# Polysketch attention with an exact-GELU MLP: every engine put into written order, and the opening laid out anew

## Chip, cores, metric

One core of one Trainium2 chip. The metric is the device time of one launch in microseconds, in medians of several runs. Each ratio is to runs of the kernel before on the same chip in the same rounds. A difference in us between two changed kernels is one of medians; a1, a2, b1 and b2 ran on another chip than the other experiments, but the kernel before took 338.88 us on the one and 338.78 to 338.85 on the other.

## The reference, cut to what matters

```python
def _attn_ref(q, k, v, S1, S2):                 # batch 4, heads 4, seq 1088, head_dim 32, r = 8
    def phi(x):                                 # 64 features: products of two 8-wide sketches
        a = np.einsum('rd,bhsd->bhsr', S1, x)
        b = np.einsum('rd,bhsd->bhsr', S2, x)
        return np.einsum('bhsi,bhsj->bhsij', a, b).reshape(*x.shape[:-1], r * r)
    q_p, k_p = (phi(q), phi(k))
    kv = np.einsum('bhsf,bhsd->bhfd', k_p, v)   # the key sums
    z = np.sum(k_p, axis=2)
    num = np.einsum('bhsf,bhfd->bhsd', q_p, kv)
    den = np.einsum('bhsf,bhf->bhs', q_p, z)[..., None] + 1e-06
    return (num / den).astype(np.float32)       # the division
# then x (4352 x 128): h = x @ w_in (128 x 2048); g = exact gelu(h); out = g @ w_out (2048 x 128)
```

The weights and sketches come as 64-bit floats and are converted on the chip by integer arithmetic ("conversion" below).

## The kernel before, in the parts that the argument touches

The 1088 tokens of each batch are two main chunks of 512 positions and a remainder of 64. There are nine chunks in all (the ninth holds the remainders). The MLP takes a chunk in 16 steps; a step is one hidden product, one gelu and one output product. Attention of the next chunk and the keys of the next batch are placed in slots between the steps.

TensorE (PE) makes the matrix products and transposes; VectorE (DVE), ScalarE (ACT) and GpSimd (POOL) do the elementwise work; SyncE (SP) issues loads. The results of TensorE land in PSUM banks and are copied or multiplied out of them. Names in the profiles: kT is a tile of transposed keys, from which and from the sketches (S) TensorE makes the key features, k_p; "expand" makes the query sketches (w_ps<-qT,Srep), whose products are q_pT (ACT copies one factor, A_sb, out of PSUM for that); kz or kv are the key sums; den is the denominator; xT is the divided, transposed attention output that the hidden products read. A pass is one of the two instructions of an fp32 product. At full pace the two passes of a 128x512 product take 0.86 us; "half pace" is about 1.8 us for the same.

```python
        def transposes(srcs):                       # keys: transpose, then copy out of PSUM on DVE
            ...
            nc.vector.tensor_copy(out=T["kT"][:, :n * 128], in_=ps[:, :n * 128])
        def features(n, pair=None):                 # needs kT
            ps = work_bank()
            for i in range(n):
                nc.tensor.matmul(ps[:, i * 64:(i + 1) * 64], lhsT=T["kT"][:, i * 128:(i + 1) * 128],
                                 rhs=S12.rearrange("p h r -> p (h r)"), start=True, stop=True)
            ...
        def num_over_den():                         # the division, features on the partitions
            ...
            for h in range(H):
                nc.scalar.activation(out=den[h * D:(h + 1) * D, :W], in_=banks[r][at:at + D, :W],
                                     func=ACT.Copy, bias=1e-6)
            nc.vector.reciprocal(out=den[:, :W], in_=den[:, :W])          # 128x512
            for h in range(H):
                nc.vector.tensor_mul(out=xT[n][rows, :W], in0=banks[h % 2][rows, :W], in1=den[rows, :W])
    ...
    for f in key_stages(0) + chunk_queries(0):
        f()
    round_bits(w_in_sb[0])                          # eight DVE instructions for each weight tile
    ...  # in the loop: chunk n+1's three query stages in slots 1, 3, 6; the next batch's keys from slot 7
```

This is the order as written. In the kernel before it isn't what runs: the framework's scheduler reorders each engine's instructions.

## Time and profile before

| | kernel before |
|---|---|
| time, median of 4 runs | 338.91 us (338.67 to 338.97) |
| span of the profiled run | 337.1 us |
| first hidden product starts | 41.93 us |
| TensorE without any gap | 70.6 to 331 us |

The profile is read by stretch: where TensorE is busy without a gap at full pace, nothing but less TensorE work helps; where it has gaps, the engine named as the releaser sets the time. The lines are in the prediction below. "PEld" is the weight load, "x8" counts instructions, and the bracket at the end of a line is the idle time before it and who ended it.

### The profile page before, as it was taken

The page shows a single profiled execution, that of the slowest core. Times are in us where ns is not written, and L with a number is a line of the kernel's source. Part 1 is how long each engine was busy: PE and PEld are TensorE (multiplying, and loading weights), DVE is VectorE, ACT ScalarE, POOL GpSimd, SP SyncE. Part 2 cuts the span into 40 slices and gives each one's busy share as a digit, 9 for nine tenths or more (in the row PEclk, how much of TensorE's full clock was granted, in tenths as well). Part 3 has the DMA queues.
Part 4 walks back from the last instruction along what each step waited for, and adds up shares of the span by engine and source line. Part 5 has one row for each costly group of instructions (what it writes and reads, how often), then busy time and mean ns, then how long its engine had stood idle before and what let it go on. Part 6 is the DMA issues. An engine that isn't in the chain of part 4 may idle for free.

```text
span 337.1 us, 2831 instructions
## 1 busy us (share of the span) xinstructions
PE 308.6 (92%) x1059; PEld 154.9 (46%) x1059; DVE 150.8 (45%) x276; ACT 125.4 (37%) x227; POOL 6.0 (2%) x21
## 2 busy tenths in 40 slices
PE   1895099799999999999999999999999999999993
PEld 1881033356434444664344435744444344444682
DVE  2348999994347054723470249124522470430101
ACT  1003137213273346222553373125533643443340
POOL 2002000000000000000000000000000000000000
PEclk9999999979999999999999999999999999999998
DMA  5999400000000000000000000000000000000000
GB/s 154 296 370 348 128 0 0 0 0 2 31 1 0 0 33 0 0 1 2 31 0 0 31 2 0 0 0 34 0 0 20 13 0 0 31 0 2 0 31 16
DMA packets 13852, 13.29 MB, mean 39 GB/s; under 512 B 3856, under 2 KB 12304, under 8 KB 13840
## 3 DMA queue, kind: packets, MB, share of 16 engines
q1 hardware_dynamic: 13840, 13.13, 12.0%
q8 instruction: 8, 0.13, 0.1%
q14 instruction: 4, 0.03, 0.0%
HBM read 10.90 MB, written 2.23 MB: 39 GB/s over the span
## 4 chain that ended last, share of the span: by engine, by line
PE 84%; DVE 13%; DMA 1%; issue 0%; SPq 0%; ACT 0%; DVEq 0%
PE o_ps L334 34%; PE h_ps L325 32%; PE kv_ps L216 6%; PE w_ps L193 3%; PE w_ps L267 3%; DVE q_pT L280 2%; PE w_ps L288 2%; DVE den L296 2%; PE w_ps L345 2%; DVE bits_e L123 1%; DVE bits_m L118 1%; PE w_ps L259 1%; PE w_ps L186 1%; DMA raw_SR<-in_S_dram 1%; DVE bits_e L122 1%; DVE xT L300 1%
## 5 line engine op out<-in xcount | busy, mean ns | idle before, releaser
L325 PE MATMUL h_ps<-xT,w_in 128*128 128x512 f32 (+1 forms) x288 | 143.3, 583 | 8.2 <-DVE xT L300 8.0
L334 PE MATMUL o_ps<-g,w_out 128*128 128x512 f32 (+1 forms) x288 | 142.7, 580 | 2.0 <-DVE w_out L124 2.0
L328 ACT ACTIVATE g<-h_ps 128x512 f32<-128x512 f32 (+1 forms) x144 | 82.4, 574 | 153.3 <-PE h_ps L325 151.7
L325 PEld LDWEIGHTS h_ps<-xT,w_in 128*128 128x128 f32 x288 | 54.6, 193 | 68.7 <-issue 49.6
L334 PEld LDWEIGHTS o_ps<-g,w_out 128*128 128x128 f32 x288 | 51.5, 191 | 55.0 <-issue 49.5
L296 DVE RECIPROCAL den<-den 128x512 f32<-128x512 f32 (+1 forms) x9 | 28.6, 3174 | 33.3 <-ACT den L294 33.3
L280 DVE TENSOR_TENSOR q_pT<-A_sb,w_ps 64x256 f32<-64x256 f32 x64 | 27.1, 424 | 18.3 <-ACT A_sb L273 17.0
L261 DVE COPY qT<-w_ps 128x512 f32<-128x512 f32 (+1 forms) x9 | 6.0, 662 | 54.1 <-PE w_ps L259 54.0
L273 ACT COPY A_sb<-w_ps 64x512 f32<-64x512 f32 (+1 forms) x36 | 19.1, 553 | 17.5 <-PE w_ps L267 10.3
L300 DVE TENSOR_TENSOR xT<-w_ps,den 32x512 f32<-32x512 f32 (+1 forms) x36 | 23.6, 657 | 0.9
L294 ACT ACTIVATE den<-w_ps 32x512 f32<-32x512 f32 (+1 forms) x36 | 20.3, 565 | 6.7 <-PE w_ps L288 6.3
L216 PEld LDWEIGHTS kv_ps<-v_aug,k_p 128*128 128x128 f32 x128 | 19.6, 226 | 6.8 <-issue 5.2
L216 PE MATMUL kv_ps<-v_aug,k_p 128*128 128x66 f32 x128 | 19.4, 305 | 0.4 <-DVE k_p L204 0.4
L338 DVE COPY o_sb<-o_ps 128x512 f32<-128x512 f32 (+1 forms) x9 | 6.0, 662 | 26.8 <-PE o_ps L334 26.8
L204 DVE TENSOR_TENSOR k_p<-a_t,w_ps 128x256 f32<-128x256 f32 x32 | 11.7, 416 | 11.4 <-ACT a_t L197 11.3
L288 PE MATMUL w_ps<-q_pT,kz 64*64 64x512 f32 (+1 forms) x96 | 10.8, 523 | 3.8 <-DVE q_pT L280 3.8
L193 PEld LDWEIGHTS w_ps<-S,kT 128*128 128x128 f32 x68 | 10.7, 233 | 5.6 <-DVE kT L188 4.0
L193 PE MATMUL w_ps<-S,kT 128*128 128x64 f32 x68 | 11.4, 318 | 1.3 <-DVE kT L188 1.3
L197 ACT COPY a_t<-w_ps 128x128 f32<-128x128 f32 (+1 forms) x10 | 2.5, 249 | 26.4 <-PE w_ps L193 26.4
L267 PE MATMUL w_ps<-qT,Srep 32*128 32x512 f32 (+1 forms) x72 | 10.8, 671 | 0.0
L188 DVE COPY kT<-w_ps 128x512 f32<-128x512 f32 (+1 forms) x10 | 6.1, 610 | 7.1 <-PE w_ps L186 7.0
L347 DVE COPY oT<-w_ps 128x512 f32<-128x512 f32 (+1 forms) x9 | 6.0, 662 | 6.5 <-PE w_ps L345 6.5
(54 smaller groups left out, 94.2 us busy)
## 6 DMA issues: line engine op xcount, KB each, us to landing
k<-in_k_dram SPq DMA_DIRECT2D x4, 512.0 KB, 9.3
v<-in_v_dram SPq DMA_DIRECT2D x4, 512.0 KB, 8.8
q<-in_q_dram SPq DMA_DIRECT2D x4, 512.0 KB, 9.7
raw_w_in<-in_moe_w_in_dram SPq DMA_DIRECT2D x4, 512.0 KB, 7.2
raw_w_out<-in_moe_w_out_dram SPq DMA_DIRECT2D x4, 512.0 KB, 8.1
out_dram<-oT SPq DMA_DIRECT2D x8, 256.0 KB, 2.0
k_rem<-in_k_dram SPq DMA_DIRECT2D x4, 32.0 KB, 3.8
v_rem<-in_v_dram SPq DMA_DIRECT2D x4, 32.0 KB, 2.4
```

The lines of the kernel that those rows point to most:

```text
L193: nc.tensor.matmul(ps[:, i * 64:(i + 1) * 64], lhsT=T["kT"][:, i * 128:(i + 1) * 128], rhs=S12.rearrange("p h r -> p (h r)"), start=True, ...
L216: nc.tensor.matmul(T["kv"][:, hp * 2 * C:(hp + 1) * 2 * C], lhsT=lhs[:, hp * 128:(hp + 1) * 128], rhs=rhs[:, 2 * hp:2 * hp + 2, :], start= ...
L267: nc.tensor.matmul(banks[g][:, :W], lhsT=Srep[rows].rearrange("p a i j -> p (a i j)"), rhs=T["qT"][rows, :W], start=True, stop=True)
L273: nc.scalar.copy(out=A[F:, :W], in_=banks[g][:F, :W])
L280: nc.vector.tensor_mul(out=qp[r * F:(r + 1) * F, :, g * 128:(g + 1) * 128], in0=a3[:, r::2, :], in1=b3[:, r::2, :])
L288: nc.tensor.matmul(banks[r][c * F:(c + 1) * F, c0:c1], lhsT=kz[b][r * F:(r + 1) * F, c, :], rhs=T["qp"][r * F:(r + 1) * F, c, c0:c1], star ...
L294: nc.scalar.activation(out=den[h * D:(h + 1) * D, :W], in_=banks[r][at:at + D, :W], func=ACT.Copy, bias=1e-6)
L296: nc.vector.reciprocal(out=den[:, :W], in_=den[:, :W])
L300: nc.vector.tensor_mul(out=xT[n][rows, :W], in0=banks[h % 2][rows, :W], in1=den[rows, :W])
L325: nc.tensor.matmul(ps[:, :W], lhsT=w_tile(w_in_sb, fi), rhs=xT[n][:, :W], start=True, stop=True)
L328: nc.scalar.activation(out=g_of[n, fi][:, :W], in_=ps[:, :W], func=ACT.Gelu)
L334: nc.tensor.matmul(o_of[n][:, :W], lhsT=w_tile(w_out_sb, fi), rhs=g_of.pop((n, fi))[:, :W], start=(fi == 0), stop=(fi == NF - 1))
```

## The change

Its intent: start the MLP sooner, and keep the scheduler from reordering DVE's queue in the first 70 us. Every engine now runs in written order. Sketches, the keys' remainder and the first queries load on ACT's queue; keys go by head pair; the first two chunks are divided by token, which needs only small reciprocals, and their MLP steps are interleaved four by four; the conversion is five DVE instructions and two of ACT. Four smaller parts: POOL makes the sketch copies and two of the first key products, each key batch's sums are one burst, the PSUM banks are shared out anew, and the remainders load in two issues in place of four. The diff, cut to its core:

```diff
+class InOrder:
+    def __getattr__(self, name):
+        op = getattr(self.engine, name)
+        return lambda *a, **k: self.tc.keep_in_program_order(op(*a, **k))
...
+    pe, dve, act, pool, sp = (InOrder(tc, e) for e in (nc.tensor, nc.vector, nc.scalar, nc.gpsimd, nc.sync))
...
+        act.dma_start(out=S_dst[i * R:(i + 1) * R, :].rearrange("r (h d) -> r h d", h=H), ...)
+    load_main(sp, "k", 0, 0, 2)
+    load_main(sp, "k", 0, 2, 4)
+    load_rem(act, "k")
+    load_main(act, "q", 0)
+    load_main(sp, "v", 0)
...
+        if helped:                                   # conversion: two of seven instructions on ACT
+            act.activation(out=low, in_=lo, func=ACT.Copy, scale=2.0 ** -52)
+            ts(out=e, in0=hi, scalar1=20, scalar2=0x7FF, op0=AX.logical_shift_right, op1=AX.bitwise_and)
+            act.activation(out=r, in_=e, func=ACT.Relu, scale=2.0 ** 23, bias=below[:rows])
+        ts(out=a, ...); stt(out=m, in0=a, scalar=2.0 ** -20, in1=low, ...)
+        stt(out=e, ...); dve.tensor_mul(out=dst, in0=m, in1=e.bitcast(FP))
...
+    query_expand(0)                                  # the opening, in written order
+    ps = work_bank()
+    for hp in range(NP):
+        kv_sum(0, ps, hp)
+    kv_sum_rem(0, ps)
+    ...                                              # two ACT copies into kv0
+    query_turn(1, hidden_bank(), by_act)
+    round_bits(w_in_sb[0], 0, 256)
+    attend_by_token(0, [out_bank(), out_bank()])
+    turn_x(0, hidden_bank(), by_act)
+    query_expand(1)
...
+    steps = [(n, fi) for f in range(0, NF, 4) for n in range(2) for fi in range(f, f + 4)]
+    steps += [(n, fi) for n in range(2, NCHUNK) for fi in range(NF)]
...
+    at(0, round_bits, w_out_sb[0], 0, 256)
+    at(1, round_bits, w_in_sb[0], 256, 256)
+    at(2, lambda: attend_by_token(1, [work_bank(), work_bank()]))
+    at(3, lambda: turn_x(1, work_bank(), by_act))
+    at(3, round_bits, w_out_sb[0], 256, 256)
+    for i in range(1, d_ff // LC):
+        at(8 * i - 3, round_bits, w_in_sb[i])
+        at(8 * i - 1, round_bits, w_out_sb[i])
+    for b in range(1, B):
+        t = NCH * b * NF
+        at(t - 24, widen_v, b)
+        for hp in range(NP):
+            at(t - 23 + 2 * hp, turn_keys, b, hp)    # transposes, kT copy on DVE
+            at(t - 22 + 2 * hp, features, b, hp)
+        if b == 1:
+            at(t - 19, turn_keys_rem, b)
+            at(t - 18, features_rem, b)
+        at(t - 16, finish_keys, b)
+    for n in range(2, NCHUNK):
+        t = n * NF
+        at(t - 13, turn_queries, n)
+        at(t - 12, query_expand, n)
+        at(t - 8, attend, n)
```

## The prediction

> **What bounds the kernel now.** I read the busy time by stretch first, then the time lines of each engine. The columns of the stretches are: width, busy us (and instructions) of PE, PEld, DVE, ACT and POOL, granted clock, DMA share, GB/s.
>
> ```profile
> 0.00:41.90 41.90, 21.33 (x88) 16.12 (x88) 24.74 (x56) 6.57 (x12) 4.92 (x19) 1.00 0.83 261
> 41.90:70.60 28.70, 26.48 (x65) 10.24 (x66) 28.33 (x56) 11.63 (x20) 0.00 (x0) 0.95 0.00 0
> 70.60:331.00 260.40, 260.38 (x906) 128.38 (x905) 96.90 (x164) 107.22 (x195) 1.10 (x2) 1.00 0.02 9
> 331.00:337.10 6.10, 0.44 (x2) 0.20 (x2) 0.85 (x2) 0.00 (x0) 0.00 (x0) 0.73 0.08 22
> ```
>
> From 70.6 to 331 us TensorE has no gap: 260 us that only less TensorE work would shorten. So everything to be won lies in the first 70 us: 41.9 us before the first hidden-layer matmul, then 28.7 us in which DVE is full (28.33 of 28.70) with the weight conversion and TensorE works below its pace. That pace, in the chain of work in order of time, is 0.86 us for the two passes of one 128x512 product, so 1.72 us for a step of one hidden and one output product. The TensorE time line of the start:
>
> ```profile
> 19.96 3.52 PE L216 MATMUL kv_ps<-v_aug,k_p 128*128 128x66 f32 x16
> 23.41 1.12 PE L216 MATMUL kv_ps<-v_rem_aug,k_p_rem 64*128 64x66 f32 x4
> 24.46 2.09 PE L267 MATMUL w_ps<-qT,Srep 32*128 32x512 f32 x8
> 30.33 2.52 PE L288 MATMUL w_ps<-q_pT,kz 64*64 64x512 f32 x8 [3.78 <-DVE q_pT L280]
> ...
> 41.93 5.40 PE L325 MATMUL h_ps<-xT,w_in 128*128 128x512 f32 x6 [8.03 <-DVE xT L300]
> 47.17 1.02 PE L334 MATMUL o_ps<-g,w_out 128*128 128x512 f32 x2
> 48.03 1.02 PE L325 MATMUL h_ps<-xT,w_in 128*128 128x512 f32 x2
> ...
> 66.42 1.12 PE L334 MATMUL o_ps<-g,w_out 128*128 128x512 f32 x2 [1.97 <-DVE w_out L124]
> 67.38 1.69 PE L325 MATMUL h_ps<-xT,w_in 128*128 128x512 f32 x2
> 68.87 1.91 PE L334 MATMUL o_ps<-g,w_out 128*128 128x512 f32 x2
> ```
>
> Until about 47 us TensorE runs at half pace, though the granted clock reads 1.00: the eight L267 passes take 2.09 us here and 1.14 us at 48.98, six hidden passes 5.40 us. The 1.97 us idle at 66.4 us, waiting for a converted weight, is followed by 3.4 us at half pace. In the second stretch these are lost: 2.7 (slow first passes) + 2.2 (idle) + 2.0 (slow again) = 6.9 us.
>
> **What the Trainium skill says.** "TensorE: Matmul & The Clock Gate", Part 1, says that TensorE starts at half clock, needs about 3.4 us of sustained work to reach full clock, and falls back after an idle window of about 3.4 us. The trace agrees on the length (3.4 us slow after the gap), but a gap of 1.97 us was enough, and 7.4 us of unbroken transposes and key sums (19.1 to 26.5) did not warm it. Part 1's "Engine queue depths" says that only TensorE looks ahead, and only for weight loads, while ACT and DVE are strict FIFO: the written order is what they run, and no trace so far contradicts it. "GPSIMD Engine Reference" § 3.1 measures a two-input fp32 product of 2048 elements at 4497 ns, so I estimate about 1.1 us for each of the two 512-element products that move to POOL; the trace has none. "DMA: Bandwidth & Descriptors", "Issuing engines are not separate DMA queues", says that a second issuing engine saves issue time only.
>
> **The change, part by part.**
>
> *Two queues and the key order.* The sketch matrices now leave first, on ACT's queue; before they were the second load and landed at 5.2 us. I give 1.2 us. SyncE no longer spends 5.3 us (eight issues of 0.67 us) on the small remainders ahead of the query load. Rounding of SR stays eight small DVE instructions, 1.7 us, so features can start near 7 us, before 9.2.
>
> *The opening in written order*, at the slow pace of the old trace. Features of pair 0: 8 passes, 2.0, to 9; query transposes 0.9; features of pair 1: 2.0, to 11.5; remainder transpose and features with their copies 1.2, to 12.7; expand 2.1, to 14.8. Expand now precedes the key sums, so the eight q_pT products (8 x 0.445 = 3.6 us, DVE) lie beside them. The key sums take their PSUM bank from expand's first, free near 14.8: 32 passes x 0.235 + 4 x 0.28 = 8.5, to 23.3. Then two ACT copies and the transposes of chunk 1: 1.0. Division by token: 16 passes of 66 columns, as key sums 3.8, to 28.1. DVE then needs, for its last bank, an add, a small reciprocal and one 128x256 product, some 0.8 us, in place of ACT den 2.4 + reciprocal 3.35 + xT 2.8 = 8.5 us. Four transposes 1.0, to 29.9, and the expand of chunk 1 stands in order ahead of the first hidden product: 2.1, **to 32 us**. Gain at that mark: 41.9 - 32 = 9.9 us.
>
> *Shorter conversion, interleaved chunks.* Per weight tile DVE falls from 5 x 0.34 + 3 x 0.60 = 3.5 us to 2 x 0.34 + 3 x 0.60 = 2.5 us, two passes of 0.6 us go to ACT, and each tile lasts eight steps (13.7 us) where it lasted four. DVE stops being the bound. But at the start DVE runs the eight products of chunk 1 (to about 35) before two half tiles (2 x 1.45): the third hidden product cannot start before 37.7, the second ends at 35.5. With the slow pace around that gap and the 16 short passes of chunk 1's division, I charge 7 us (5 to 10), where the old kernel lost 6.9. So interleaving gains little net.
>
> *Dense work.* From the old loop: 331.0 - 41.9 = 289.1, less 6.9 lost = 282.2; chunk 1's transposes, expand and attend (2.5) leave, its division by token and transposes (2.2) come: **282 us**. Keys do the same passes.
>
> *Program order everywhere.* This I take as the costly part. Attend of chunk 2b-1 stands at step 32b-24; the transposes of batch b's keys at 32b-23, their features at 32b-22. For b = 2 and 3 both meet. The DVE time line of the old kernel at that place:
>
> ```profile
> 132.21 3.35 DVE L296 RECIPROCAL den<-den 128x512 f32<-128x512 f32 x1 [4.66 <-ACT den L294]
> 135.60 0.69 DVE L188 COPY kT<-w_ps 128x512 f32<-128x512 f32 x1
> 136.20 2.78 DVE L300 TENSOR_TENSOR xT<-w_ps,den 32x512 f32<-32x512 f32 x4
> ```
>
> The old schedule slipped the kT copy between reciprocal and products and let TensorE run two more steps before the features (136.34, which is 7.7 us after attend began at 128.65). In written order the kT copy stands behind both: attend 1.1 + den 2.4 + reciprocal 3.35 + xT 2.8 + copy 0.7 = 10.4 us after attend begins. TensorE is there after attend 1.0 + transposes 0.44 + four products at 0.86 = 4.9 us, and cannot pass. **Idle 5.5 us, twice**, and after each some 2 us of slow pace, as at 67 us: 15 us. For batch 1 the remainder's copy stands behind a tile's conversion at the same step, which waits for ACT: about 2 us once.
>
> *Sum.* 32 + 282 + 7 + 15 + 2 = 338; the end (o_sb copy, transposes, store) is unchanged, 6.1: span 344 us; measured time is 1.75 us above the span (338.85 against 337.1): **346 us** with the waits, **331** if the 15 us do not appear.
>
> **The rivals.** *First: the order waits are not there or shrink.* For it: whoever placed the steps by hand may have looked for just such gaps. Against: DVE is a queue, and the copy is written behind the reciprocal. Time: 331, and 327 if the opening also starts at 29. *Second: the half pace is worse than I reckon.* The key sums of a batch become one burst of 36 short passes (36 x 0.108 = 3.9 us); such passes did not warm TensorE before, so a burst could count as idle and slow the next 3.4 us. Against: 2.6 us of key passes and features at 141.4 left the clock at full. Three times 1.7 us: up to 351. *Third: the opening waits for POOL or a load.* POOL's products have 6.6 us of room before the second half of the key sums, and v landed at 7.1 before; it would move 32 by at most 3 us.
>
> **Range and chances.** I give the waits 65%: 346, give or take 5. Without them 331, give or take 4. 0.65 x 346 + 0.35 x 331 = 340.75; I say **341 us**, range **326 to 350**. Over 2% faster means below 332.1: most of the half of the second case, and a little of the first if the opening is much better: 0.30. Within 2% (332.1 to 345.6): 0.45. Slower: 0.25.
>
> **What would show it.** First hidden product at 30 to 34 us; key sums still near 0.23 us a pass, with q_pT beside them; no 3.35 us reciprocal before it. DVE no longer full from 40 to 70. Two TensorE gaps of about 5.5 us ahead of key features, released by the DVE copy of kT, at steps 42 and 74 (near 122 and 197 us: 32, plus 1.72 us a step and what is placed between), each followed by a lower granted clock. If TensorE is as unbroken after 70 us as now, the order part is wrong and the time is near 331. If the first hidden product comes after 36, the opening part is wrong.

## The result, and the profile after

**Slower by 4.3%:** 353.41 us (352.69 to 353.66, 4 runs) against 338.91; the ratio is 1.0426, with a 95% interval of 1.0408 to 1.0444. Ratios here are the mean time of one kernel's runs over the mean of the other's runs of the same rounds, so not quite the ratio of the medians. The outputs are correct.

The busy time by stretch of the changed kernel, cut where its gaps are (columns as in the prediction; rows of full pace and the end left out):

```profile
0.00:34.30 34.30, 24.93 (x108) 20.02 (x108) 10.85 (x33) 8.21 (x17) 9.34 (x37) 1.00 1.01 316
34.30:51.60 17.30, 11.45 (x39) 6.20 (x35) 10.02 (x30) 7.65 (x16) 0.00 (x0) 0.80 0.02 4
51.60:131.00 79.40, 76.75 (x256) 36.47 (x257) 38.65 (x69) 35.82 (x65) 1.10 (x2) 1.00 0.02 7
131.00:150.00 19.00, 13.58 (x44) 7.50 (x43) 10.03 (x11) 4.98 (x10) 0.00 (x0) 0.82 0.00 0
...
208.00:228.00 20.00, 14.57 (x44) 8.08 (x44) 10.05 (x11) 4.88 (x11) 0.00 (x0) 0.83 0.00 0
...
```

The MLP starts at 34.35 us, where it started at 41.93. But TensorE, which had no gap after 70.6 us, now has two of more than 5 us, one in 131 to 150 and one in 208 to 228, and each of these stretches has a granted clock near 0.82. TensorE's six longest waits, summed over the run (engine, tile, whom it waited for: us in total, times, longest):

```profile
PE w_ps L24 <- DVE kT L24: 10.8, 2, 5.4
PE h_ps L24 <- DVE w_in L24: 6.3, 2, 5.3
PE h_ps L24 <- DMA k<-in_k_dram: 4.0, 1, 4.0
PE h_ps L24 <- DMA q<-in_q_dram: 1.9, 1, 1.9
PE w_ps L24 <- DVE kT_rem L24: 1.7, 1, 1.7
PE w_ps L24 <- ACT A_sb L24: 1.6, 1, 1.6
```

All lines carry L24, the line of the in-order helper, so one goes by tiles. The first of the two kT gaps, in TensorE's and then DVE's time line:

```profile
129.56 1.09 PE L24 MATMUL w_ps<-q_pT,kz 64*64 64x512 f32 x8
...
133.70 1.02 PE L24 MATMUL h_ps<-xT,w_in 128*128 128x512 f32 x2
140.15 1.97 PE L24 MATMUL w_ps<-S,kT 128*128 128x64 f32 x8 [5.42 <-DVE kT L24]
141.91 2.02 PE L24 MATMUL o_ps<-g,w_out 128*128 128x512 f32 x2
143.72 1.69 PE L24 MATMUL h_ps<-xT,w_in 128*128 128x512 f32 x2
```
```profile
133.12 3.35 DVE L24 RECIPROCAL den<-den 128x512 f32<-128x512 f32 x1 [6.39 <-ACT den L24]
136.58 2.79 DVE L24 TENSOR_TENSOR xT<-w_ps,den 32x512 f32<-32x512 f32 x4
139.40 0.69 DVE L24 COPY kT<-w_ps 128x512 f32<-128x512 f32 x1
```

The kT copy stands behind the reciprocal and the products, as written. The transposes that it copies began at 132.4; DVE stood idle 6.39 us before 133.12, waiting in order for den. After the gap the features take 1.97 us in place of about 1.0, and the next two products 1.8 and 1.5 us (from start to start) in place of 0.86.

**Where the time went.** I took what is lost from the time line of the profiled run, as elapsed time less the same instructions at full pace. The full-pace TensorE work that is left after the first hidden product is then the same in both kernels within 0.4 us (282.2 and 281.8):

| after the first hidden product | before | after |
|---|---|---|
| start of it | 41.93 | 34.35 |
| lost to waits and half pace in the first MLP steps | 6.9 | 9.1 |
| two kT gaps (2 x 5.42) and slow passes behind (2.4 and 3.3) | 0 | 16.6 |
| waits for the remainder's kT (1.7) and for w_in at 97 us (1.0) | 0 | 2.7 |
| end (last store) | 6.1 | 6.2 |

The differences sum to -7.6 + 2.2 + 16.6 + 2.7 + 0.1 = 14.0 us; the spans differ by 350.7 - 337.1 = 13.6. (Added again from the starts in the time line, the 6.9 of the kernel before is 6.6, which changes nothing in the argument.)

### The profile page after: what moved, and what is told of

It reads as the page before. It is cut to its first block, busy times and chain, and to the rows that moved or that the text cites. A ratio compares the mean times of both kernels' runs of the same rounds, so it can differ in the third digit from the quotient of the medians.

```text
span 350.7 us, 2876 instructions
## 1 busy us (share of the span) xinstructions
PE 315.9 (90%) x1083; PEld 164.0 (47%) x1083; DVE 130.4 (37%) x236; ACT 133.1 (38%) x247; POOL 11.5 (3%) x41
## 4 chain that ended last, share of the span: by engine, by line
PE 83%; DVE 9%; ACT 4%; DMA 2%; issue 1%; ACTq 1%; DVEq 0%
PE o_ps L24 34%; PE h_ps L24 32%; PE w_ps L24 17%; DMA q<-in_q_dram 2%; DVE den L24 2%; DVE xT L24 2%; ACT den L24 1%; DVE q_pT L24 1%; ACT A_sb L24 1%; DVE bits_e L24 1%; DVE bits_m L24 1%; ACTq L24 1%; DVE w_in L24 1%; ACT g L24 0%; ACT bits_low L24 0%
## 5 line engine op out<-in xcount | busy, mean ns | idle before, releaser
L24 PE MATMUL h_ps<-xT,w_in 128*128 128x512 f32 (+1 forms) x288 | 143.7, 582 | 6.3 <-DVE w_in L24 6.3
L24 PE MATMUL o_ps<-g,w_out 128*128 128x512 f32 (+1 forms) x288 | 144.3, 584 | 0.5 <-DVE w_out L24 0.5
L24 ACT ACTIVATE g<-h_ps 128x512 f32<-128x512 f32 (+1 forms) x144 | 82.4, 573 | 158.4 <-PE h_ps L24 158.0
L24 PEld LDWEIGHTS h_ps<-xT,w_in 128*128 128x128 f32 x288 | 55.5, 194 | 73.1 <-issue 61.6
L24 PEld LDWEIGHTS o_ps<-g,w_out 128*128 128x128 f32 x288 | 51.6, 193 | 49.6 <-issue 47.3
L24 DVE TENSOR_TENSOR q_pT<-A_sb,w_ps 64x256 f32<-64x256 f32 x68 | 28.8, 424 | 25.0 <-ACT A_sb L24 23.8
L24 DVE RECIPROCAL den<-den 128x512 f32<-128x512 f32 (+1 forms) x7 | 21.9, 3124 | 40.9 <-ACT den L24 40.9
L24 DVE COPY o_sb<-o_ps 128x512 f32<-128x512 f32 (+1 forms) x9 | 6.0, 662 | 55.9 <-PE o_ps L24 55.9
L24 PEld LDWEIGHTS w_ps<-v_aug,k_p 128*128 128x128 f32 x128 | 18.1, 227 | 4.6 <-issue 4.6
L24 ACT COPY A_sb<-w_ps 64x512 f32<-64x512 f32 (+1 forms) x36 | 17.4, 557 | 6.0 <-PE w_ps L24 6.0
L24 PE MATMUL w_ps<-v_aug,k_p 128*128 128x66 f32 x128 | 18.1, 309 | 1.6 <-ACT A_sb L24 1.6
L24 DVE TENSOR_TENSOR xT<-w_ps,den 32x512 f32<-32x512 f32 (+1 forms) x28 | 18.2, 649 | 1.0
L24 PE MATMUL w_ps<-S,kT 128*128 128x64 f32 x48 | 7.9, 321 | 10.8 <-DVE kT L24 10.8
L24 ACT ACTIVATE den<-w_ps 32x512 f32<-32x512 f32 (+1 forms) x28 | 15.6, 558 | 2.9 <-PE w_ps L24 2.6
L24 PEld LDWEIGHTS w_ps<-S,kT 128*128 128x128 f32 x48 | 7.8, 237 | 14.4 <-DVE kT L24 12.5
L24 DVE TENSOR_TENSOR k_p<-a_t,w_ps 128x512 f32<-128x512 f32 x12 | 7.7, 684 | 13.7 <-ACT a_t L24 13.7
L24 PE MATMUL w_ps<-qT,Srep 32*128 32x512 f32 (+1 forms) x72 | 11.7, 726 | 0.0
L24 DVE SCALAR_TENSOR_TENSOR bits_m<-bits_a,bits_low 128x512 f32<-128x512 uint32 (+2 forms) x11 | 6.1, 558 | 14.4 <-ACT bits_low L24 14.0
L24 DVE COPY kz<-w_ps 64x64 f32<-64x64 f32 x12 | 2.1, 218 | 21.1 <-PE w_ps L24 21.1
L24 DVE COPY qT<-w_ps 128x512 f32<-128x512 f32 (+1 forms) x7 | 4.6, 654 | 13.5 <-PE w_ps L24 13.5
L24 DVE COPY oT<-w_ps 128x512 f32<-128x512 f32 (+1 forms) x9 | 6.0, 662 | 6.5 <-PE w_ps L24 6.5
L24 ACT ACTIVATE bits_r<-bits_e,below 128x512 uint32<-128x512 uint32 (+1 forms) x10 | 6.3, 632 | 4.2 <-DVE bits_e L24 4.2
```

What stands on the lines that cost most here:

```text
L24: return lambda *a, **k: self.tc.keep_in_program_order(op(*a, **k))
```

## Experiments

The theory after the result: the gain of the opening (7.6 us) is given back by DVE's written order, in two places: the kT copy behind the division (16.6 us), and the first weights' conversion behind chunk 1's products (the 5.3 us wait for w_in). The rivals: the gaps come from a PSUM bank or the clock and not from DVE's order; or program order costs little and the new opening itself is what costs.

| run | us, median of 4 | ratio to before |
|---|---|---|
| changed kernel | 353.41 | 1.0426 |
| a1 keys four steps later | 335.94 | 0.9912 |
| a2 kT copy on ACT | 337.17 | 0.9947 |
| a3 kT copy ahead of xT | 347.50 | 1.0234 |
| b1 kernel before, written order | 383.55 | 1.1317 |
| b2 changed kernel, scheduler's order | 332.60 | 0.9820 |
| c1 = a1 + early conversion | 328.11 | 0.9686 |
| t1 = a1, chunk 0 divided by feature | 340.96 | 1.0070 |
| q1 = a1, one load queue | 336.13 | 0.9921 |
| v1 = c1, long conversion | 330.78 | 0.9772 |
| i1 = c1, chunks in turn | 327.63 | 0.9675 |
| d1 = c1 + four small moves | 323.53 | 0.9541 |
| d2 = d1, one load queue | 321.76 | 0.9501 |

All twelve runs gave correct outputs, and the kernel before took 338.78 to 338.88 us beside them.

### The two gaps: DVE's order, or something that moves along?

**a1: the keys of batches 2 and 3 four steps later.**

```diff
+        late = 4 if b > 1 else 0
         for hp in range(NP):
-            at(t - 23 + 2 * hp, turn_keys, b, hp)
-            at(t - 22 + 2 * hp, features, b, hp)
+            at(t - 23 + 2 * hp + late, turn_keys, b, hp)
+            at(t - 22 + 2 * hp + late, features, b, hp)
...
-        at(t - 16, finish_keys, b)
+        at(t - 16 + late // 2, finish_keys, b)
```

> The changed kernel with the key transposes and features of batches 2 and 3 written four steps later (and their sum two steps later); nothing else. Order theory: the two TensorE gaps of 5.4 us ahead of key features and the slow passes behind each (2.4 and 3.3 us counted from the two time lines) all vanish, 16.6 us: 353.4 to about 337. Rival (the gaps come from something that moves along with the features, such as a PSUM bank held by the division or a clock event): the gaps move along, time within 2 us of 353.

Measured: 335.94 us, 17.5 below the changed kernel. DVE's time line at the same place:

```profile
133.02 3.35 DVE L24 RECIPROCAL den<-den 128x512 f32<-128x512 f32 x1 [6.39 <-ACT den L24]
136.48 2.79 DVE L24 TENSOR_TENSOR xT<-w_ps,den 32x512 f32<-32x512 f32 x4
139.80 0.69 DVE L24 COPY kT<-w_ps 128x512 f32<-128x512 f32 x1 [0.54 <-PE w_ps L24]
```

DVE does the same three things at nearly the same times. But now DVE waits 0.54 us for TensorE's transposes, where TensorE waited 5.42 us for DVE, and TensorE's kT waits are gone from the list.

**a2: only the engine of the copy.**

```diff
-        key_turn(b, hp, work_bank(), by_dve)
+        key_turn(b, hp, work_bank(), by_act if b > 1 else by_dve)
```

> The changed kernel with the kT copies of batches 2 and 3 made by ACT in place of DVE, at the same place in the order. Order theory: only DVE's queue holds the copy back, ACT is free behind its den copies, so the gaps vanish without any step moved: about 337. Rival (bank or clock): no change, 353. Rival 2 (ACT is held too, by the four den copies of 2.4 us): a gap of about 1 us stays, no slow spell, 339.

Measured: 337.17 us, with no kT wait of TensorE left, not even the 1 us of the second rival. ACT's copy and the features at the place of the first gap:

```profile
134.98 0.58 ACT L24 COPY kT<-w_ps 128x512 f32<-128x512 f32 x1
```
```profile
135.93 1.00 PE L24 MATMUL w_ps<-S,kT 128*128 128x64 f32 x8
```

No step was moved and the banks are the same, so neither the place of the features nor a bank held by the division makes the gap: it is DVE's queue.

That a2 is 1.2 us slower than a1 does not come from the gaps: in the profiled runs it is 1.5 us behind a1 before the place of the first one, and 1.5 us at the end. With the same opening, q was used at 9.03 to 10.93 us in the profiled runs of the changed kernel, a1, a2 and a3, and the slow passes behind the wait for w_in lasted differently long; the reciprocal at the place of the first gap starts at 133.12, 133.02, 134.50 and 134.73 us. Differences of up to about 1.7 us between these four say nothing of the gaps.

**a3: the dose.** DVE alone is reordered, as the old schedule had it.

```diff
-        at(t - 8, attend, n)
+        at(t - 8, attend, n, n in (3, 5))            # up to the reciprocal
+        if n in (3, 5):
+            at(t - 7, lambda n=n: rest_of[n]())      # the xT products, behind the kT copy
```

> The changed kernel (353.4) with one thing reordered on DVE for chunks 3 and 5: the kT copy stands between the reciprocal and the xT products, as the old schedule had it; TensorE's order is untouched. Order theory, by dose: the copy is done 2.8 us earlier, so each of the two gaps shrinks from 5.4 to about 2.6 us. If a gap of that length still costs a spell of slow passes (2 to 3 us each, as the 1.97 us gap of the kernel before did): 347 to 348. If it does not: 342 to 343.

Measured: 347.50 us (344.93 to 348.04); both gaps are 2.53 us. The second one in TensorE's time line:

```profile
211.99 1.97 PE L24 MATMUL w_ps<-S,kT 128*128 128x64 f32 x8 [2.53 <-DVE kT L24]
213.76 2.02 PE L24 MATMUL o_ps<-g,w_out 128*128 128x512 f32 x2
215.57 1.92 PE L24 MATMUL h_ps<-xT,w_in 128*128 128x512 f32 x2
```

Half the gap saved only 5.9 us of the 17.5, about what the two gaps lost in length (2 x 2.89), since the slow passes came nonetheless: full pace returns only in the products from 219.26 on, 7 us after the gap (after the first gap from 143.70 on, 5 us after it).

### Program order by itself

**b1: the kernel before, with every engine in written order.** The edit is the helper class and `nc.tensor`, `nc.vector` and so on replaced by its objects.

> The kernel before with every engine in written order and nothing else changed. If program order alone costs what I think: key features stand one or two steps behind the division there as well, three gaps of 3.7 to 5.5 us with slow passes behind (some 19 us), and the first tile's conversion comes after the first division (some 4 us): about 360. Rival (program order costs little by itself, the new step plan does): 339 to 345.

Measured: 383.55 us, 44.7 above the kernel before and twice the cost that I expected. Six waits for kT sum to 23.1 us, the longest 11.9 us; the first hidden product comes at 51.72 us after a wait for w_in:

```profile
51.72 3.78 PE L24 MATMUL h_ps<-xT,w_in 128*128 128x512 f32 x4 [12.97 <-DVE w_in L24]
...
89.65 1.97 PE L24 MATMUL w_ps<-S,kT 128*128 128x64 f32 x8 [11.86 <-DVE kT L24]
```

The second is the worst case that I had left out: at batch 1 the kT copy stands behind reciprocal, xT products and the eight-instruction conversions of two whole tiles.

**b2: the changed kernel with the scheduler's order.**

```diff
-        return lambda *a, **k: self.tc.keep_in_program_order(op(*a, **k))
+        return op
```

> The changed kernel without the fixed order: the framework places the instructions itself as it did before. Order theory: the two gaps go, and the conversion at the start can slip ahead too: 330 to 338. Rival (the new opening itself is what costs): 348 to 355.

Measured: 332.60 us. From the first hidden product to the last output product TensorE's time line shows no wait. But that first product starts at 41.6 us, seven later than in written order. DVE and TensorE in the opening:

```profile
11.55 0.29 DVE L173 TENSOR_SCALAR bits_e<-raw_w_in 128x256 uint32<-128x256 uint32 x1 [6.16 <-DMA raw_w_in<-in_moe_w_in_dram]
...
12.50 0.17 DVE L193 COPY sT<-w_ps 128x16 f32<-128x16 f32 x1
```
```profile
12.98 0.47 PE L204 MATMUL h_ps<-ident,q 128*128 128x128 f32 x1 [6.21 <-ACT kT L206]
```

The scheduler put the weights' conversion ahead of the sketch copy sT, and DVE waited 6.16 us for the weights to land. It did the same on ACT: the first conversion instruction there stood 6.20 us for the same weights, ahead of the two kT copies (12.37 us). The features need both sT and kT, so no run says which of the two alone would have cost the time. For the changed kernel, then, the scheduler's order is good in the loop and bad in the opening, and the written order the reverse. That is no rule: in the kernel before, the written order was worse in the opening too (51.72 us in b1 against 41.93).

### The opening

**c1: the first conversions where DVE is idle, and by DVE alone.** On top of a1:

```diff
     query_expand(0)
+    round_bits(w_in_sb[0], 0, 256, helped=False)
+    round_bits(w_out_sb[0], 0, 256, helped=False)
+    round_bits(w_in_sb[0], 256, 256, helped=False)
     ps = work_bank()
...
-    round_bits(w_in_sb[0], 0, 256)
-    at(0, round_bits, w_out_sb[0], 0, 256)
-    at(1, round_bits, w_in_sb[0], 256, 256)
```

> The run with the later keys (335.9) plus one change: the first three half tiles of weights are converted by DVE alone right behind chunk 0's q_pT products, while TensorE sums the keys (DVE idles 6.7 us there), in place of after chunk 1's products. My theory of the opening: the 5.2 us wait for w_in ahead of the third hidden product goes, the slow passes after it shrink, and the first division no longer waits for a conversion: 6 to 8 us, about 329. Rival (TensorE is at half pace there anyway and the wait only overlaps it): 2 us or less, 334.

Measured: 328.11 us, 7.8 below a1. The first MLP steps in TensorE's time line, a1 and then c1:

```profile
32.44 2.86 PE L24 MATMUL h_ps<-xT,w_in 128*128 128x512 f32 x4
40.47 2.04 PE L24 MATMUL h_ps<-xT,w_in 128*128 128x512 f32 x2 [5.17 <-DVE w_in L24]
42.31 3.52 PE L24 MATMUL w_ps<-kv,q_pT 128*128 128x66 f32 x16
45.62 2.02 PE L24 MATMUL o_ps<-g,w_out 128*128 128x512 f32 x2
```
```profile
33.53 3.91 PE L24 MATMUL h_ps<-xT,w_in 128*128 128x512 f32 x6
37.28 1.90 PE L24 MATMUL w_ps<-kv,q_pT 128*128 128x66 f32 x16
39.02 1.08 PE L24 MATMUL o_ps<-g,w_out 128*128 128x512 f32 x2
```

c1's load of q landed a microsecond later, so it starts later, and still has its first output product 6.6 us earlier: the wait is gone, and without it the 16 division passes and the output product run at full pace. Two things changed at once, the place of the three conversions and that ACT no longer helps in them; no run parts them.

**t1: chunk 0 divided as before the change.** On top of a1:

```diff
-    attend_by_token(0, [out_bank(), out_bank()])
-    turn_x(0, hidden_bank(), by_act)
+    fill_kz(0, kv0.rearrange("p n c -> p (n c)"), by_pool)
+    attend(0)
     query_expand(1)
-    fill_kz(0, kv0.rearrange("p n c -> p (n c)"), by_pool)
```

> The run with the later keys (335.9) with chunk 0 divided as in the kernel before (four den copies, the 3.35 us reciprocal, four products), chunk 1 still by token. If the division by token is what brought the first hidden product forward: it comes 3 to 6 us later (8.5 us of ACT and DVE against 16 more short passes, two short DVE chains and four transposes with their copy): 339 to 342. Rival (the wait for the converted weights hides the difference, as DVE reaches it at a fixed time): within 1.5 us of 335.9.

Measured: 340.96 us, 5.0 above a1. The first hidden product comes at 39.72 us, where a1 has it at 32.44; a part is regained because the wait for w_in then is 2.56 us in place of 5.17. The division of chunk 0 by token is worth 5 us beside a1's wait. (Here POOL fills kz just ahead of the division, where the kernel before used DVE, so the edit isn't quite the old state.)

**q1: one load queue.** On top of a1 the three loads on ACT's queue go to SyncE's (`act` becomes `sp` in the three calls).

> The run with the later keys (335.9) with all loads on SyncE's queue, sketches still first, then the keys' remainder and q in the written order. If the second queue matters: the sketches come as soon but the key halves are issued after them, 1 us later, and v and weights 2 to 3 us later: 337 to 339. Rival (issue time is hidden): within 1 us of 335.9.

Measured: 336.13 us, the same as a1's 335.94. The second queue brings nothing here: the first keys are used at 4.32 us (one queue) against 3.6 to 4.0 (two, in all profiled runs), but the sketches at 2.75 against 3.6 to 4.2, and q at 8.65 against 9.0 to 10.9 (a1: 9.03).

**v1 and i1: the shorter conversion and the interleaving, each undone in c1.** For v1 the default becomes `helped=False`. For i1:

```diff
-    steps = [(n, fi) for f in range(0, NF, 4) for n in range(2) for fi in range(f, f + 4)]
-    steps += [(n, fi) for n in range(2, NCHUNK) for fi in range(NF)]
+    steps = [(n, fi) for n in range(NCHUNK) for fi in range(NF)]
-        at(8 * i - 3, round_bits, w_in_sb[i])
-        at(8 * i - 1, round_bits, w_out_sb[i])
+        at((1, 4, 8)[i - 1], round_bits, w_in_sb[i])
+        at((2, 6, 10)[i - 1], round_bits, w_out_sb[i])
```

(with w_out's second half at step 0, the division of chunk 1 at step 5 and its transposes at step 11)

> The early-conversion run (328.1) with the conversion lengthened again to eight DVE instructions for every tile, no help of ACT (3.5 us of DVE for 2.5). If the shorter conversion is what makes DVE keep up in the interleaved part: waits for w_in and w_out return, 331 or more. Rival (interleaving leaves DVE so much room that its length no longer matters; and ACT's helper steps had themselves to wait behind gelu): 326.5 to 329.5.

Measured: 330.78 us, 2.7 above c1, just below the 331 that I had named as its sign. Two waits behind conversions grow: kT_rem from 1.68 to 2.32 us and w_in from 0.97 to 2.19, 1.9 us of the 2.7; where the rest goes was not looked for.

> The early-conversion run (328.1) with chunks 0 and 1 one after the other in place of interleaved, the conversions placed for that twice as dense. If interleaving is needed: a tile's conversion (2.5 us, two tiles each 6.9 us, plus keys and the division of chunk 1) falls behind and TensorE waits for weights, 331 to 336. Rival (with the shorter conversion DVE keeps up anyway): 327 to 330.

Measured: 327.63 us, no different from c1's 328.11 within the noise (0.9675, 0.9658 to 0.9691, against 0.9686, 0.9672 to 0.9701), with three short waits of 0.7 to 1.5 us. The interleaving isn't needed once the first conversions stand right.

### The best version

**d1** and **d2**, on top of c1:

```diff
-    load_rem(act, "k")
-    load_main(act, "q", 0)
+    load_main(act, "q", 0)
+    load_rem(act, "k")
...
-    ps = work_bank()                 # key sums of batch 0
+    ps = hidden_bank()
...
+        at((5, 13, 17)[i - 1], round_bits, w_in_sb[i])    # now written behind the keys' slots
+        at((7, 15, 21)[i - 1], round_bits, w_out_sb[i])
```

> The run with early conversion plus four small ones: q issued ahead of the keys' remainder, the key sums in a hidden bank in place of one that expand still holds (1.6 us wait seen), the remainder's transposes of batch 1 written ahead of the conversion at the same step (1.7 us wait), the last tile's conversion three or four steps earlier (1.0 us wait). All waits gone: 4 to 6 us below the early-conversion run, about 324. If the waits only move: within 1.5 us of it.

Measured: 323.53 us, 4.6 below c1. The waits for A_sb (1.6 us), for batch 1's kT_rem (1.7) and for w_in (1.0) are gone from the list; one of 1.1 us for den_tok is new. The four moves were not tried one by one.

> The fastest run so far (323.5) with all loads on SyncE's queue. In the one-queue run q came at 8.65 us, 1.5 us earlier than with two queues, but a later wait for weights swallowed it. With that wait gone it should show: 322 to 323. If the first keys and sketches, issued later, cost as much: 323.5 to 324.5.

Measured: **321.76 us** (321.65 to 322.42), 5.0% faster than the kernel before (0.9501, 0.9487 to 0.9515) and 9% below the changed kernel. The first hidden product comes at 30.57 us. One queue saves 1.8 us here: q is used at 8.18 us, where d1's profiled run has it at 10.26. That it shows here and not in q1 because the wait for weights is gone is the likely reason, but not shown: a1's profiled run had q as early as 9.03, so that q1 had little to win there. The waits of TensorE that are left, apart from the loads at the start:

```profile
PE h_ps L24 <- DVE den_tok L24: 1.0, 1, 1.0
PE w_ps L24 <- DVE o_sb L24: 0.9, 2, 0.5
PE o_ps L24 <- DVE w_out L24: 0.5, 1, 0.5
PE h_ps L24 <- DVE kT_rem L24: 0.4, 1, 0.4
```

## Why the prediction was wrong

- **What bounds the kernel: right.** Everything to be won lay in the first 70 us, and the dense work is equal: 344.5 (end of the last output product) less 34.35 and less the 28.4 us lost leaves 281.8; I had reckoned 282.
- **The order waits: right in place and mechanism, under-sized by 1.6 us.** Predicted 5.5 us idle twice ahead of the key features, released by the kT copy, and 2 us slow after each, 15 in all; measured 5.42 twice and 2.4 and 3.3. a1, a2 and a3 show the cause.
- **The steps that failed: the sizes of the opening's terms, and the weight.** The point of 341 us was 12.4 too low. Of this, 7.4 us are in the sum with the waits itself (346, "give or take 5"): "to 32 us" was 34.35 (2.35), "I charge 7 us" was 9.1 (2.1), the order waits 1.6, batch 1 0.7, and the time above the span 0.9, less 0.2 in the dense work. The other 5 us are "I give the waits 65%": averaging with 331 pulled the point down to 341 and the range's end to 350, within its own 346 plus 5. For the rival that the waits "are not there or shrink" I had only a guess about whoever placed the steps; against it stood the written order and three durations from the trace. In the changed kernel nothing shrank (5.42 for 5.5). But full weight alone would not have been enough.
- **The opening: right in kind, 4.5 us too good.** Two terms of "to 32 us" failed, and quicker passes hid a part. q was used at 10.93 us, after a wait of 1.9 us, so expand ended at 16.93, not 14.8. And the key sums' bank was free at 18.56, another 1.6 us later, not with expand's end: the first passes into the four banks run side by side and so do the second (14.84 to 16.08 and 15.86 to 16.93), all four banks are complete within 0.02 us, and only then does the first ACT copy start (16.95), behind which stand DVE's first two products. The key sums so began 3.8 us late; their passes and those of the division took less than reckoned and won 1.4 back. "I charge 7 us" was 9.1: the third hidden product waited 5.3 us for w_in, not 2.2, as chunk 1's products started only at 35.05, behind expand's ACT copies once more, and each half tile took 1.83 us (38.56 to 40.39), not 1.45. c1, in which this wait is gone, is 7.8 us faster than a1.
- **Slips in its sums.** Features of pair 1 end at 11.9 by its own terms (9 + 0.9 + 2.0), not 11.5; 35 + 2 x 1.45 is 37.9, not 37.7; the slow passes after the old kernel's gap are about 1.7 us, not 2.0 (67.38 to 70.57 is 3.2 us, not 3.4). None is above 0.4 us.
- **"About 2 us once" for batch 1:** 1.7, plus a wait of 1.0 for w_in at 97 us that I had not seen.
- **The time above the span:** I added 1.75 us; the profiled run (352.69 against a span of 350.7) shows 2.0, and the median is 0.7 above that run.
- **The parts of the change:** the sketches did come 1.1 us earlier (4.19 against 5.32), for which I gave 1.2, but that is their place in the order of issue: on one queue they come at 2.7. The second queue itself is worth nothing (q1) or costs 1.8 us (d2). The division of chunk 0 by token brings 5.0 us (t1) and the shorter conversion 2.7 (v1). That "interleaving gains little net" held (i1). The head pairs alone were not tried.
- **The rivals:** the burst of key sums did not slow TensorE: after the 36 passes at 77.24 to 81.37 us the next product runs at 0.9 us. POOL's two products were in time; they took 2.09 us, 1.05 each, where the estimate from the Trainium skill, "GPSIMD Engine Reference" § 3.1, was 1.1. The third rival, an opening that waits for a load, came half true: not v but q, by 1.9 us.

## What to carry to other kernels

Before an engine is put into written order, go through every slot in which two of its customers meet, and add up what stands in that queue ahead of the instruction that TensorE waits for next. A copy of 0.69 us behind a reciprocal and four products cost two gaps and 17 us here, and moving it four steps, or to another engine, gave this back. If the durations on the path are in the trace, give that sum its full weight; and then look for what it leaves out, here a load that came 1.9 us late and a PSUM bank that was still held.

## What the Trainium skill lacked or had wrong

- "TensorE: Matmul & The Clock Gate", Part 1, and its table of rules warn of idle gaps of about 3 us and more. Here gaps of 2.53 us (a3) and of 1.97 us (kernel before) already brought a spell of half pace, of up to 6 us. The length of the gap alone doesn't decide: after gaps of 1.98 and 2.17 us in b1 (at 60.67 and 70.34 us) the passes ran at full pace.
- The same part says that about 3.4 us of sustained work reaches full clock. In the changed kernel the passes from 18.56 to 30.7 us follow each other without a gap and stay at half pace: 32 passes of 66 columns in 7.06 us and, after four more and four transposes, 16 in 3.63, where 16 take 1.90 at full pace (c1 at 37.28). Part 4 of the page says this of transposes; for passes of few columns it doesn't. The granted clock reads 1.00 through that stretch, so take the pace from the passes; the same Part 1 warns that the clock's trace events are unreliable.
- The same page's Part 3 says that passes with 32 rows each run side by side in different row groups. The trace agrees (eight expand passes in 2.09 us at half pace, four and four together, where two full 128x512 passes took about 1.8). What the page doesn't draw from this is the consequence: all four banks come free together, at 16.91 to 16.93 us, so the copies out of them can't begin while expand still runs, and the next user of a bank waits (1.63 us here).
